# Second layer's straight path as one nest of arms with one packed control word; the gate of the token-order unit one unit earlier, its product by halves

## The chip, the core and the metric

The kernel runs on one core of one Trainium2 chip. The time is the device time in microseconds of one execution, as the median over runs; the trace is one profiled execution of the same program. The engines are named as in the trace: PE (TensorE matmuls), PEld (its weight loads), DVE (VectorE), ACT (ScalarE), POOL (GpSimd) and SP (SyncE, which issues DMAs). A "q" behind the name means the engine's sequencer, which runs ahead of the engine's array and carries out register loads, branches and semaphore waits.

## The reference

```
def reference(**kwargs):
    ...
    attn_out = _attn_ref(**attn_kwargs)              # 2 x 8 heads, 768 positions, width 64
    x = ... .reshape(B * S, H * D)                   # 1536 tokens x 512
    x = _moe_ref(x=x, **moe_kwargs)                  # max of three products, then w_out
    return _moe2_ref(x=x, **moe2_kwargs)

def _moe2_ref(x, w_skip, w_gate, w1, w2):
    do_compute = x @ w_skip > 0
    out = x.copy()
    xc = x[do_compute]
    logits = xc @ w_gate                             # 8 experts, one per token (argmax)
    ...
    for e in range(E):
        h = np.maximum(xc[mask] @ w1[e], 0.0)
        y[mask] = gate_w[mask, None] * (h @ w2[e])
    out[do_compute] = xc + y
    return out.astype(np.float32)
```

Attention with a window of 16 and pooled keys, a first layer ("max of three products"), and a second layer in which each token that is not skipped goes through one of eight experts. How many tokens an expert gets is known only when the chip has computed the logits.

## The kernel before

The first 293 us of the trace are attention and the first layer, in an order that a planner (`arrange`) worked out beforehand; the change leaves that order alone. What follows is the second layer. Routing (`route`, `route2`, `route3`) writes each token's number and gate into a table in HBM, sorted by expert; `counts` sums the experts' tokens on PE and leaves the sums in PSUM. From them `steps()` in `plan()` (lines 628 to 705, one-partition instructions on DVE, spread over the first unit) works out integers in the tile `ints`: how many units each expert has, where they begin, and two flags. `reg()` loads one integer from `ints` into a register, by default on all five engines.

Work is done in units. `pair(p, t)` takes 256 tokens through the expert whose weights lie in slot `p`: the first product `first(f)` (12 matmuls of 128x256 for each of 8 pieces), relu on ACT and its low part `htl` on DVE, and the second product `second(f)` (6 matmuls of 128x512). `begin` copies the token numbers and rows on POOL, `end` does the last sum on DVE and scatters rows with POOL's indirect DMA, `tail_x` and `tail` treat up to 32 tokens of a further expert beside a pair. `single(p, t)` takes 128 tokens: 24 matmuls of 128x512 into `ph[0]` and `ph[1]` (line 1187), four transposes for each half (`turn_h`, line 1193), 24 matmuls of 128x512 into `py[0]` (line 1221). With `dense` it is the token-order unit: the last 128 tokens in their own order (`turn_d`, `put_d` bring them in during the single before), with a gate per token that is zero for a token that other units have done. `begin_d` makes that gate: a DVE memset of `yq`, a PE matmul of `yq` with the bounds `lim` into `pq` (line 1155), five small DVE instructions. `end_d` multiplies by the gate and stores the result in two halves from SP.

The order is written out by hand (`manual_schedule`), and branches are taken by every engine on its own registers. After the first layer:

```
    with tc.If(EA > EARLY) as early2:      # two pairs of the largest expert, whose number is guessed
        with tc.manual_schedule():
            pair(0, 0, gen=steps())
            numbers()
            pair(0, 1)
    with early2.Else():
        ...                                # the same in two smaller forms
    ...
    with tc.manual_schedule():
        with tc.If(reg(ints[:, 6 * NE:6 * NE + 1], MAXT) > 0, preferred_fallthrough_block=False) as others:
            any_ranks()                    # general form, all eight experts
        with others.Else():
            most()                         # the straight path
```

The program joins behind `early2`, loads the flag for `others` and goes into one of two arms. In `most()` the two first expert counts are loaded into registers `VK[0]` and `VK[1]`; then come a pair, a second pair, a third if `VK[0] > 6` (within it a fourth if `VK[0] > 8`), a single if `VK[0]` is even, and, after a register load of the second flag, either a single followed by the token-order unit or a single alone. Each of these `If`s has its own join; the arm in which nothing is done there waits for its engine's earlier work and adds the skipped semaphore counts, since whoever waits later must find the same count on either way.

In the profiled execution the path is: `early2` true (pairs from 295 us and from 318.7), `most` (pairs from 342.2, 371.6 and 400.1; the condition `VK[0] > 6` holds, `VK[0] > 8` does not), no single in slot 0, then the single from 425.7 and the token-order unit from 440.9. By the source, a pair has 152 matmuls, a single 56 to 64, the token-order unit 56, and each has a weight load beside it.

Of the kernel before, what the change touches and what calls it, by code (L numbers as in the profile page):

```python
# [40 lines left out]
BIG = 1 << 20  # L41
NCH = 16
MAXT = NT
NRAW = 4
NCON = 293
NG9 = 10
# [99 lines left out]
def build(tc, a, out):  # L146
# [376 lines left out]
    def route2(u):  # L523
        acc = ACC[u]
        if u == NG - 1:
            ST["cnt"], ST["cntp"] = counts(ACC[NG], ST["part"])
        oh, ohb, do, w, tab = ST["rt", u]

        def be(z):
            return z.unsqueeze(1).broadcast_to([P, TPG, NE])  # L530
        pp = psM.tile([P, 512], F32, name="pm")
        for j in range(TPG):
            o = pp[:, j * NE:(j + 1) * NE]
            nc.tensor.matmul(o, tri, ohb[:, j, :], start=True, stop=False)
            for i in range(j):
                nc.tensor.matmul(o, ones, ohb[:, i, :], start=False, stop=False)
            nc.tensor.matmul(o, ones, acc, start=False, stop=True)
        ST["pp", u] = pp

    def route3(u):  # L540
        oh, ohb, do, w, tab = ST["rt", u]
        pp = ST["pp", u]

        def be(z):
            return z.unsqueeze(1).broadcast_to([P, TPG, NE])
        nc.vector.tensor_tensor(w, pp[:, :TPG * NE].rearrange("p (t e) -> p t e", e=NE), be(iocap), ALU.add)
        nc.vector.tensor_tensor(w, w, oh, ALU.mult)
        sl = tp.tile([P, TPG], F32, name="rsl")
        nc.vector.tensor_reduce(sl, w, AX.X, ALU.add)
        nc.vector.tensor_scalar(do, do, -float(BIG), float(BIG), ALU.mult, ALU.add)  # L550
        si = tp.tile([P, TPG], I32, name="rsi")
        nc.vector.tensor_tensor(si, sl, do, ALU.add)  # L552
        ST["si", u] = si

    def scatter(u, j):
        tab, si = ST["rt", u][4], ST["si", u]
# [3 lines left out]
    def counts(*accs):  # L560
        pc = psM.tile([P, 512], F32, name="pm")
        for i, acc in enumerate(accs):
            nc.tensor.matmul(pc[:1, i * NE:(i + 1) * NE], ones[:, :1], acc, start=True, stop=True)
        return [pc[:1, i * NE:(i + 1) * NE] for i in range(len(accs))]

    def count3():
        ST["c3"] = counts(ACC[NG - 1])[0]

    ONE = {}

# [30 lines left out]
    def plan():  # L601
# [5 lines left out]
        n, used, u1, rank, n0, nk, ek, bk, uk, pk, rb, xk, kc = T.values()  # L607
        dn, lim = pk, kc[:, :2]
        ci = mp.tile([1, NE], I32, name="p_ci")
        ints = mp.tile([1, 6 * NE + 2], I32, name="p_ints")  # L610
        ONE["lim"] = lim
        hq, hqt = M2["hq"]
        m, m2 = (z[:1, SEQ * NE:].rearrange("p (a b) -> p a b", b=NE) for z in (hq, hqt))
# [14 lines left out]
        def steps():  # L628
# [38 lines left out]
            V.tensor_copy(fs[:, 3:4], xk[:, 3:4])  # L667
            V.tensor_scalar(fs[:, 4:5], ONE["ge2"], -1.0, float(EARLY), ALU.mult, ALU.add)
            V.tensor_reduce(fr, fs, AX.X, ALU.max)
            V.tensor_copy(ints[:, 6 * NE:6 * NE + 1], fr)  # L670
            yield
            V.tensor_reduce(dn[:, 0:1], dn, AX.X, ALU.add)
            V.tensor_scalar(fr, fr, 0.0, None, ALU.is_equal)
            V.scalar_tensor_tensor(fr, nk[:, 1:2], 0.0, fr, ALU.is_gt, ALU.mult)
            V.tensor_tensor(fr, fr, dn[:, 0:1], ALU.mult)
            V.tensor_copy(ints[:, 6 * NE + 1:], fr)
            V.tensor_tensor(nk[:, 0:1], nk[:, 0:1], fr, ALU.subtract)
            V.tensor_tensor(dn[:, 1:2], nk[:, 0:1], ONE["ge2"], ALU.add)
            V.tensor_tensor(dn[:, 1:2], dn[:, 1:2], ONE["ge"], ALU.add)
            V.tensor_scalar(lim[:, 1:2], ek[:, 0:1], float(CAP), None, ALU.mult)  # L680
# [460 lines left out]
        end(2)  # L1141

    def turn_d():
        for c in range(KC1):
            o = slice(c * P, (c + 1) * P)
            nc.tensor.transpose(ptx[0][:, o], X2[NG - 1, TPG - 1][:, o], ident)  # L1146
# [3 lines left out]
        nc.scalar.copy(xth[:, :, :P], src)  # L1150
        nc.vector.tensor_tensor(xtl[:, :, :P], src, xth[:, :, :P].bitcast(F32), ALU.subtract)

    def begin_d():
        nc.vector.memset(yq[:1], 1.0)  # L1154
        nc.tensor.matmul(pq[:, :2], yq[:1], ONE["lim"], start=True, stop=True)  # L1155
        nc.vector.tensor_copy(gd[0], ST["si", NG - 1][:, TPG - 1:])  # L1156
        nc.vector.tensor_tensor(gd[1], gd[0], pq[:, 0:1], ALU.is_ge)
        nc.vector.tensor_tensor(gd[2], gd[0], pq[:, 1:2], ALU.is_lt)
        nc.vector.tensor_tensor(gd[1], gd[1], gd[2], ALU.mult)
        nc.vector.tensor_tensor(gd[1], gd[1], ST["rt", NG - 1][4][:, TPG - 1, 1:2].bitcast(F32), ALU.mult)  # L1160

    def end_d():
        rows = out[B * S - P:, :]
        nc.sync.dma_start(xr[1], rows)
        for z in (slice(0, DM // 2), slice(DM // 2, DM)):
            nc.vector.scalar_tensor_tensor(yo[0][:, z], py[0][:, z], gd[1], xr[1][:, z], ALU.mult, ALU.add)  # L1166
            nc.sync.dma_start(rows[:, z], yo[0][:, z])

    def single(p, t, spl=0, last=False, hr=HR, then=False, dense=False):
        if dense:  # L1170
            begin_d()
        else:
            begin(1)
        if spl:
            tail_x(spl)
        todo = list(range(NCH)) if spl else []
        pth = [ph[2], ph[0]]

        def splits(n):
            for _ in range(min(n, len(todo))):  # L1180
                split(todo.pop(0), 1 - p)

        def first(hf, ds):
            for d in ds:
                wh, wl = M2["w", p, 2 * d + hf]
                for n, (l, r) in enumerate(((xth, wh), (xth, wl), (xtl, wh))):
                    nc.tensor.matmul(ph[hf], l[:, d, :P], r, start=(d == 0 and n == 0), stop=(d == KC1 - 1 and n == 2))  # L1187
            if ds[-1] == KC1 - 1:
                nc.scalar.activation(hr[hf], ph[hf], AF.Relu)

        def turn_h(i):
            for c in range(4):
                nc.tensor.transpose(pth[i][:, c * P:(c + 1) * P], hr[i][:, c * P:(c + 1) * P], ident)  # L1193
            nc.scalar.copy(hth[i], pth[i])
            nc.vector.tensor_tensor(htl[i], pth[i], hth[i].bitcast(F32), ALU.subtract)

        first(0, [0, 1, 2, 3])
        splits(4)
        first(1, [0, 1])
        turn_h(0)  # L1200
        splits(2)
        first(1, [2, 3])
        splits(2)
        for f in range(8):
            wh, wl = M2["w", p, 8 + f]
            i, o = f // 4, f % 4 * P
            if f == 2:
                turn_h(1)
                if not last:
                    turn_x()  # L1210
                elif then:
                    turn_d()
                splits(4)
            if f == 3:
                if not last:
                    next_x(t + 2)
                elif then:
                    put_d()
                splits(4)
            for n, (l, r) in enumerate(((hth[i], wh), (hth[i], wl), (htl[i], wh))):  # L1220
                nc.tensor.matmul(py[0], l[:, o:o + P], r, start=(f == 0 and n == 0), stop=(f == 7 and n == 2))  # L1221
            if spl and f >= 4:
                tail(f - 4)
        if dense:
            end_d()
        else:
            end(1)

    def nothing(p, t, spl=0):
        if spl:  # L1230
# [7 lines left out]
        for c in range(NCH):  # L1238
            raw_load(c, reg(ints[:, NE + 1:NE + 2], NE - 1, **SP))

    take_x()
    with tc.If(EA > EARLY) as early2:
        with tc.manual_schedule():
            pair(0, 0, gen=steps())
            numbers()
            pair(0, 1)
    with early2.Else():
        ids("in2", reg(ONE["r0"], NROW - 2 * P, **SP))
        with tc.If(EA > 0) as early:
            with tc.manual_schedule():  # L1250
                pair(0, 0, gen=steps())
        with early.Else():
            for _ in steps():
                pass
            advance(row(1))
            turn_x()
            next_x(2)
        numbers()
    VK, EK, BK, LK, MR = {}, {}, {}, {}, {}

    def head(k, body, t):
# [14 lines left out]
    def run_rank(k):  # L1276
# [15 lines left out]
        if k + 1 < NE:  # L1292
            with tc.If(VK[k + 1] > 0):
                run_rank(k + 1)
    def most():

        for k in range(2):
            VK[k] = reg(ints[:, k:k + 1], MAXT + 1)
        b0, b1, l0 = (reg(ints[:, i * NE + k:i * NE + k + 1], 14, **SP) for i, k in ((2, 0), (2, 1), (3, 0)))
        MR[1], MR[2] = (reg(ints[:, 5 * NE + k:5 * NE + k + 1], NROW - P, **SP) for k in (1, 2))  # L1300
        e2 = reg(ints[:, NE + 2:NE + 3], NE - 1, **SP)
# [2 lines left out]
        for c in range(NCH):  # L1304
            raw_load(c, e2)
        pair(0, b0 + 2, FAST2)
        with tc.If(VK[0] > 6):
            pair(0, b0 + 3)
            with tc.If(VK[0] > 8):
                pair(0, b0 + 4)  # L1310
        with tc.If((VK[0] & 1) == 0):
            single(0, l0, hr=M2["raw"])
        with tc.If(reg(ints[:, 6 * NE + 1:], 1) > 0) as dense:
            single(1, b1 + 1, last=True, hr=M2["raw"], then=True)
            single(0, 0, last=True, hr=M2["raw"][2:], dense=True)
        with dense.Else():
            with tc.If(VK[1] > 1):
                single(1, b1 + 1, last=True, hr=M2["raw"])

    def any_ranks():  # L1320
        for k in range(NE):
# [2 lines left out]
                z[k] = reg(ints[:, i * NE + k:i * NE + k + 1], m, **SP)  # L1324
        run_rank(0)

    with tc.manual_schedule():
        with tc.If(reg(ints[:, 6 * NE:6 * NE + 1], MAXT) > 0, preferred_fallthrough_block=False) as others:
            any_ranks()
        with others.Else():  # L1330
            most()
    ctx.close()


# [61 lines left out]
```

## Time and profile before

| | us |
|---|---|
| median of 3 runs | 461.05 |
| lowest, highest | 458.27, 465.42 |
| the profiled execution | 461.48 |
| its span, first to last instruction | 459.6 |

The profiled execution's time is its span and 1.9 us around it. Of the span PE is busy 432.6 us (94%), DVE 245.7, ACT 197.2 and POOL 128.9. In rows of a timeline the columns are start, duration, engine, line, operation, output and inputs, and in brackets the idle time before and what ended it; starts are us from the span's beginning.

### The profile page before, as it was taken

What the parts mean: (1) busy time and instruction counts of PE and PEld (TensorE: products, weight loads), DVE (VectorE), ACT (ScalarE), POOL (GpSimd) and SP (SyncE); (2) the same over time, 40 slices, a digit from 0 to 9 for tenths busy, and PEclk for the clock granted to TensorE, in tenths of its full rate; (3) what the DMA queues carried; (4) which work ended last, traced back from release to release, by engine and by line L of the source; (5) the groups of instructions that cost most, each with busy time, mean ns of one, the idle gap of its engine ahead of it and who ended that gap; (6) DMA issues with size and microseconds to landing.
All of it is one profiled execution on the core that took longest, in us unless ns stands there. A gap on an engine that the chain in (4) does not pass through costs nothing. (4 is left out here: it accounts for less than half of the span.)

```text
span 459.6 us, 9467 instructions
## 1 busy us (share of the span) xinstructions
PE 432.6 (94%) x3426; PEld 387.2 (84%) x3426; DVE 245.7 (53%) x783; ACT 197.2 (43%) x522; POOL 128.9 (28%) x177
## 2 busy tenths in 40 slices
PE   7987799999999999999999999999998999998994
PEld 3556689899989899999999988998997889797773
DVE  4998999989963343445114174587136541313121
ACT  2799987756364472357221173211115511111210
POOL 2343453322121441423102511142224033232200
PEclk9999989999999999999999999999999999999899
DMA  8994625575525254220030290312941381010110
GB/s 245 269 271 167 239 103 183 181 244 202 178 85 193 100 189 118 49 82 22 3 134 5 61 348 7 137 11 79 345 121 51 117 297 49 25 50 2 48 49 30
DMA packets 28168, 58.46 MB, mean 127 GB/s; under 512 B 6163, under 2 KB 8723, under 8 KB 28104
## 3 DMA queue, kind: packets, MB, share of 16 engines
q1 hardware_dynamic: 25544, 51.71, 34.6%
q0 software_dynamic: 2560, 5.96, 4.1%
q8 instruction: 32, 0.52, 0.5%
q14 instruction: 32, 0.26, 0.2%
HBM read 48.16 MB, written 10.47 MB: 128 GB/s over the span
## 5 line engine op out<-in xcount | busy, mean ns | idle before, releaser
L367 PE MATMUL pm<-xh,wh 128*128 128x384 f32 x288 | 66.1, 349 | 3.2 <-DVE t L376 2.0
L367 PE MATMUL pm<-xh,wl 128*128 128x384 f32 x288 | 63.1, 339 | 0.0
L367 PE MATMUL pm<-xl,wh 128*128 128x384 f32 x288 | 63.1, 339 | 0.0
L367 PEld LDWEIGHTS pm<-xh,wh 128*128 128x128 f32 x288 | 49.4, 189 | 5.3 <-DVE t L376 2.5
L1106 ACT ACTIVATE hth<-ph 128x256 fp32r<-128x256 f32 x40 | 15.3, 384 | 89.5 <-PE ph L1103 72.2
L367 PEld LDWEIGHTS pm<-xh,wl 128*128 128x128 f32 x288 | 51.7, 190 | 0.5 <-DVE wl L360 0.5
L367 PEld LDWEIGHTS pm<-xl,wh 128*128 128x128 f32 x288 | 51.9, 190 | 0.0
L376 DVE TENSOR_TENSOR t<-pm,t 128x384 f32<-128x384 f32 x48 | 26.5, 553 | 37.8 <-PE pm L367 30.1
L1107 DVE SCALAR_TENSOR_TENSOR htl<-ph,hth 128x256 fp32r<-128x256 f32 x40 | 16.7, 422 | 55.5 <-ACT hth L1106 55.5
L287 POOL TENSOR_TENSOR pr<-pr,se 128x360 f32<-128x360 f32 x32 | 26.2, 823 | 68.9 <-DVE se L283 44.6
L394 PE MATMUL pm<-wh,h 128*128 128x262 f32 (+1 forms) x288 | 42.8, 288 | 1.3 <-ACT v L214 1.0
L277 ACT ACTIVATE pr<-pr,mx 128x120 f32<-128x120 f32 x96 | 36.6, 384 | 10.9 <-DVE mx L271 10.8
L384 POOL TENSOR_TENSOR h<-t,h 128x384 fp32r<-128x384 f32 x24 | 26.1, 1093 | 48.9 <-ACT h L381 47.4
L394 PEld LDWEIGHTS pm<-wh,h 128*128 128x128 f32 x288 | 37.9, 190 | 2.1 <-ACT v L214 1.3
L1115 PE MATMUL pm<-wh,htl 128*128 128x512 f32 x80 | 31.5, 394 | 1.3 <-DVE htl L1107 1.3
L1115 PE MATMUL pm<-wh,hth 128*128 128x512 f32 x80 | 31.8, 397 | 0.0
L1115 PE MATMUL pm<-wl,hth 128*128 128x512 f32 x80 | 31.4, 392 | 0.0
L557 POOL DMA_INDIRECT table<-rtab,rsi x12 | 11.9, 995 | 58.9 <-DVE rsi L552 38.9
L342 POOL TENSOR_SCALAR cx<-cx 128x512 f32<-128x512 f32 x24 | 18.3, 764 | 35.5 <-ACT cx L334 33.8
L736 POOL DMA_INDIRECT xn<-x2d,inx x14 | 14.9, 1063 | 46.0 <-DVE xm L1069 30.4
L381 ACT CAST h<-t 128x384 fp32r<-128x384 f32 x24 | 11.9, 513 | 35.2 <-DVE t L376 33.9
L1103 PE MATMUL ph<-xth,wh 128*128 128x256 f32 x160 | 26.4, 287 | 0.0
(338 smaller groups left out, 856.6 us busy)
## 6 DMA issues: line engine op xcount, KB each, us to landing
raw<-in_m SPq DMA_DIRECT2D x48, 256.0 KB
raw<-in_wx SPq DMA_DIRECT2D x22, 512.0 KB
kx<-in_kx SPq DMA_DIRECT2D x12, 360.0 KB
vx<-in_vx SPq DMA_DIRECT2D x14, 288.0 KB
qt<-in_qt SPq DMA_DIRECT2D x16, 192.0 KB
x2d<-raw SPq DMA_DIRECT2D x12, 256.0 KB
raw<-in_kt SPq DMA_DIRECT2D x7, 384.0 KB
raw<-in_vt SPq DMA_DIRECT2D x7, 384.0 KB
```

Source lines behind the costliest of these rows:

```text
L277: nc.scalar.activation(pr[:, t, :], pr[:, t, :], AF.Exp, bias=mx[:, t:t + 1], scale=-1.0, accum_out=se[:, t:t + 1])
L287: nc.gpsimd.tensor_tensor(pr, pr, se.unsqueeze(2).broadcast_to([P, TPG, KT]), ALU.mult)
L342: nc.gpsimd.tensor_scalar(x, x, HIGH, LOW, ALU.min, ALU.max)
L367: nc.tensor.matmul(ST["ch", u, f, j], l[j, f][:, c * P:(c + 1) * P], r[u][:, c, :], start=(cs[0] == 0 and n == 0), stop=(cs[-1] == KC1 - 1 ...
L376: nc.vector.tensor_tensor(ST["t1", u, f], ps, ST["t1", u, f], ALU.max)
L384: nc.gpsimd.tensor_tensor(HL[u, f], ST["t1", u, f], HH[u, f].bitcast(F32), ALU.subtract)
L394: nc.tensor.matmul(ps, l[u, f][:, t * P:(t + 1) * P], r[3, f][:, lo:hi], start=(part != 1 and n == 0), stop=(part != 0 and n == len(ops) - 1))
L736: nc.gpsimd.indirect_dma_start(out=xn[t], out_offset=None, in_=x2d, in_offset=bass.IndirectOffsetOnAxis(ap=inx[:, t, 0:1], axis=0), bounds ...
L1103: nc.tensor.matmul(ps, w[:, o:o + P], r[:, d, :], start=(n == 0), stop=(n == 3 * KC1 - 1))
L1106: nc.scalar.activation(hh, ps, AF.Relu)
L1107: nc.vector.scalar_tensor_tensor(hl, ps, 0.0, hh.bitcast(F32), ALU.max, ALU.subtract)
L1115: nc.tensor.matmul(py[i], l[:, o:o + P], r, start=(f == 0 and n == 0), stop=(f == 7 and n == 2))
```

## The change

`counts` returns one row of PSUM, and `route3` of the last group copies the sums into SBUF (one DVE copy). `steps()` no longer writes two flags but one word: the number of the largest expert's remaining units in the low five bits, 32 if the second expert has a full unit, 64 if the token-order unit is to run, 128 for the general form. The word is loaded once into all engines. The choice between `any_ranks` and `most` now stands inside the true arm of `early2`, without a join between; its Else part gets an `any_ranks` of its own. Inside `most` each `If` has its continuation within both arms, so the code of the later units is there several times: `last()` holds the single and the token-order unit (or the single alone), `odd()` a single and `last()`, or `last()` alone, and `odd()` stands behind the fourth pair, in the Else of the fourth, and in the Else of the third. The memset of `yq` moves into `turn_d`, the rest of `begin_d` becomes `gate_d` and is called behind `put_d` in the single before. The token-order unit's second product is done in two column halves of 256 (48 matmuls for 24): for f = 0 to 3 both halves by turns, then f = 4 to 7 of the first half, its sum and store, then the same for the second.

```diff
 ... (counts, count3: one row of PSUM is returned)
@@ route3
+        if u == NG - 1:
+            cs = w.rearrange("p t e -> p (t e)")[:1, :2 * NE]
+            nc.vector.tensor_copy(cs, ST["cnt"])
+            ST["cnt"], ST["cntp"] = cs[:, :NE], cs[:, NE:]
@@ steps
-            V.tensor_copy(ints[:, 6 * NE:6 * NE + 1], fr)
             yield
             V.tensor_reduce(dn[:, 0:1], dn, AX.X, ALU.add)
-            V.tensor_scalar(fr, fr, 0.0, None, ALU.is_equal)
-            V.scalar_tensor_tensor(fr, nk[:, 1:2], 0.0, fr, ALU.is_gt, ALU.mult)
-            V.tensor_tensor(fr, fr, dn[:, 0:1], ALU.mult)
-            V.tensor_copy(ints[:, 6 * NE + 1:], fr)
-            V.tensor_tensor(nk[:, 0:1], nk[:, 0:1], fr, ALU.subtract)
+            V.tensor_scalar(fs[:, 0:1], fr, 0.0, None, ALU.is_equal)
+            V.scalar_tensor_tensor(fs[:, 0:1], nk[:, 1:2], 0.0, fs[:, 0:1], ALU.is_gt, ALU.mult)
+            V.tensor_tensor(fs[:, 0:1], fs[:, 0:1], dn[:, 0:1], ALU.mult)
+            V.tensor_tensor(nk[:, 0:1], nk[:, 0:1], fs[:, 0:1], ALU.subtract)
+            V.tensor_scalar(fr, fr, 0.0, float(OTHER), ALU.is_gt, ALU.mult)
+            V.scalar_tensor_tensor(fr, fs[:, 0:1], float(DENSE), fr, ALU.mult, ALU.add)
+            V.tensor_scalar(fs[:, 1:2], nk[:, 1:2], 0.0, float(ONES), ALU.is_gt, ALU.mult)
+            V.tensor_tensor(fr, fr, fs[:, 1:2], ALU.add)
+            V.scalar_tensor_tensor(ints[:, 6 * NE:], nk[:, 0:1], 1.0, fr, ALU.mult, ALU.add)
@@ turn_d, begin_d, end_d
     def turn_d():
+        nc.vector.memset(yq[:1], 1.0)
         for c in range(KC1):
...
-    def begin_d():
-        nc.vector.memset(yq[:1], 1.0)
+    def gate_d():
         nc.tensor.matmul(pq[:, :2], yq[:1], ONE["lim"], start=True, stop=True)
...
+    halves = [slice(0, DM // 2), slice(DM // 2, DM)]
+
+    def second_d(z, f):
+        wh, wl = M2["w", 0, 8 + f]
+        h, o = f // 4, f % 4 * P
+        for n, (l, r) in enumerate(((hth[h], wh), (hth[h], wl), (htl[h], wh))):
+            nc.tensor.matmul(py[z][:, halves[z]], l[:, o:o + P], r[:, halves[z]],
+                             start=(f == 0 and n == 0), stop=(f == 7 and n == 2))
+
     def end_d():
         rows = out[B * S - P:, :]
         nc.sync.dma_start(xr[1], rows)
-        for z in (slice(0, DM // 2), slice(DM // 2, DM)):
-            nc.vector.scalar_tensor_tensor(yo[0][:, z], py[0][:, z], gd[1], xr[1][:, z], ALU.mult, ALU.add)
-            nc.sync.dma_start(rows[:, z], yo[0][:, z])
+        for z, cs in enumerate(halves):
+            for f in range(4, 8):
+                second_d(z, f)
+            nc.vector.scalar_tensor_tensor(yo[0][:, cs], py[z][:, cs], gd[1], xr[1][:, cs], ALU.mult, ALU.add)
+            nc.sync.dma_start(rows[:, cs], yo[0][:, cs])
@@ single
-        if dense:
-            begin_d()
-        else:
+        if not dense:
             begin(1)
...
+            if dense and f == 4:
+                end_d()
+                return
             if f == 3:
                 if not last:
                     next_x(t + 2)
                 elif then:
                     put_d()
+                    gate_d()
                 splits(4)
+            if dense:
+                for z in range(2):
+                    second_d(z, f)
+                continue
@@ most
-    def most():
-        for k in range(2):
-            VK[k] = reg(ints[:, k:k + 1], MAXT + 1)
+    def most(w):
...
-        with tc.If(VK[0] > 6):
+        def last():
+            with tc.If((w & DENSE) > 0, preferred_fallthrough_block=True) as dense:
+                single(1, b1 + 1, last=True, hr=M2["raw"], then=True)
+                single(0, 0, last=True, hr=M2["raw"][2:], dense=True)
+            with dense.Else():
+                with tc.If((w & ONES) > 0):
+                    single(1, b1 + 1, last=True, hr=M2["raw"])
+
+        def odd():
+            with tc.If((w & 1) > 0) as one:
+                single(0, l0, hr=M2["raw"])
+                last()
+            with one.Else():
+                last()
+
+        with tc.If((w & (ONES - 1)) > 5, preferred_fallthrough_block=True) as four:
             pair(0, b0 + 3)
-            with tc.If(VK[0] > 8):
+            with tc.If((w & (ONES - 1)) > 7, preferred_fallthrough_block=True) as five:
                 pair(0, b0 + 4)
-        with tc.If((VK[0] & 1) == 0):
-            single(0, l0, hr=M2["raw"])
-        with tc.If(reg(ints[:, 6 * NE + 1:], 1) > 0) as dense:
-            single(1, b1 + 1, last=True, hr=M2["raw"], then=True)
-            single(0, 0, last=True, hr=M2["raw"][2:], dense=True)
-        with dense.Else():
-            with tc.If(VK[1] > 1):
-                single(1, b1 + 1, last=True, hr=M2["raw"])
+                odd()
+            with five.Else():
+                odd()
+        with four.Else():
+            odd()
@@ the end of build
+    with tc.If(EA > EARLY, preferred_fallthrough_block=True) as early2:
+        with tc.manual_schedule():
+            pair(0, 0, gen=steps())
+            numbers()
+            pair(0, 1)
+            word = reg(ints[:, 6 * NE:], 2 * OTHER - 1)
+            with tc.If(word >= OTHER, preferred_fallthrough_block=False) as others:
+                any_ranks()
+            with others.Else():
+                most(word)
+    with early2.Else():
...
+        numbers()
         with tc.manual_schedule():
             any_ranks()
```

## Rows read from the trace of the kernel before

**Rows 1.** The page: engines' busy time, and one of its two instruction queues

```profile
PE 432.6 (94%) x3426; PEld 387.2 (84%) x3426; DVE 245.7 (53%) x783; ACT 197.2 (43%) x522; POOL 128.9 (28%) x177
...
q8 instruction: 32, 0.52, 0.5%
```

**Rows 2.** Timeline, DVE at the end of the first pair

```profile
318.25 1.43 DVE L1078 SCALAR_TENSOR_TENSOR yo<-pm,ic,xr 128x512 f32<-128x512 f32 x2 [0.71 <-PE pm L1115]
```

**Rows 3.** Timeline, SP, DVE and PE around the entry into `most`

```profile
341.07 0.75 SPq L1015 DMA_DIRECT2D mi<-table  x1
...
341.68 1.43 DVE L1078 SCALAR_TENSOR_TENSOR yo<-pm,ic,xr 128x512 f32<-128x512 f32 x2 [0.71 <-PE pm L1115]
...
347.75 0.21 DVE L1021 TENSOR_SCALAR mo<-mi,con 128x1 int32<-128x1 int32 x1 [4.64 <-PE pm L1115]
...
347.94 1.08 DVE L1107 SCALAR_TENSOR_TENSOR htl<-ph,hth 128x256 fp32r<-128x256 f32 x3
...
348.41 0.50 PE L1115 MATMUL pm<-wh,htl 128*128 128x512 f32 x1 [1.30 <-DVE htl L1107]
```

**Rows 4.** By line (count, duration min/median/max in ns, first and last start): early2's branches, loads

```profile
L1242 DVEq COMPARE_BRANCH  x2: 55/56/57, 296.0 to 342.4; - x2
...
L712 DVEq EVENT_SEMAPHORE  x5: 21/50/50, 346.0 to 346.9; - x5
...
L1242 PEldq COMPARE_BRANCH  x2: 92/198/304, 293.4 to 339.2; - x2
```

**Rows 5.** By line, PE's sequencer: the branches behind the last pair and the last

```profile
L1309 PEldq COMPARE_BRANCH  x2: 190/262/333, 420.7 to 424.0; - x2
...
L1311 PEldq COMPARE_BRANCH  x1: 438/438/438, 424.4 to 424.4; - x1
...
L1313 PEldq COMPARE_BRANCH  x2: 77/1736/3394, 425.4 to 450.7; - x2
```

**Rows 6.** Timeline, PE from the last pair to the first single

```profile
423.42 0.39 PE L1115 MATMUL pm<-wh,htl 128*128 128x512 f32 x1
425.65 0.47 PE L1187 MATMUL ph<-wh,xth 128*128 128x512 f32 x1 [1.84 <-DVEq L1311]
```

**Rows 7.** A stretch: us, PE busy (instructions), granted clock, DMA share, GB/s

```profile
426.80:430.10 3.30, 3.30 (x10) 0.50 0.06 25
```

**Rows 8.** The chain that ended last: start, us, what

```profile
425.65 5.97 PE ph L1187 x18
...
441.23 4.42 PE ph L1187 x18
...
449.30 4.19 PE pm L1221 x18
```

**Rows 9.** Timeline, DVE and PE around the gate

```profile
435.98 0.69 DVE L1195 TENSOR_TENSOR htl<-ph,hth 128x512 fp32r<-128x512 f32 x1 [2.53 <-ACT hth L1194]
...
436.24 0.40 PE L1221 MATMUL pm<-mw_11h,hth 128*128 128x512 f32 x1
...
439.44 0.39 PE L1221 MATMUL pm<-mw_15h,htl 128*128 128x512 f32 x1
...
440.63 0.17 DVE L1154 MEMSET yq<- 1x128 f32 x1
...
440.85 0.38 PE L1155 MATMUL pm<-p_kc,yq 1*128 1x2 f32 x2 [1.03 <-DVE mo L1156]
441.16 0.51 PE L1187 MATMUL ph<-wh,xth 128*128 128x512 f32 x1
```

**Rows 10.** Stretch, matmuls of line 1103 alone: us, PE busy (instructions), clock, DMA

```profile
318.75:323.02 4.27, 4.27 (x36) 1.00 0.72 204
```

**Rows 11.** Timeline, the end: PE, DVE, SP

```profile
453.08 0.40 PE L1221 MATMUL pm<-wh,htl 128*128 128x512 f32 x1
...
453.51 0.87 DVE L1166 SCALAR_TENSOR_TENSOR yo<-pm,mo,xr 128x256 f32<-128x256 f32 x2 [2.87 <-PE pm L1221]
454.02 1.27 SPq L1167 DMA_DIRECT2D out<-yo  x2
```

More of the change, by code (lines that the diff above doesn't have):

```diff
@@ L43 @@
 MAXT = NT
+ONES, DENSE, OTHER = 32, 64, 128
 NRAW = 4
@@ L525, in route2 @@
         if u == NG - 1:
-            ST["cnt"], ST["cntp"] = counts(ACC[NG], ST["part"])
+            ST["cnt"] = counts(ACC[NG], ST["part"])
         oh, ohb, do, w, tab = ST["rt", u]
@@ L563, in counts @@
             nc.tensor.matmul(pc[:1, i * NE:(i + 1) * NE], ones[:, :1], acc, start=True, stop=True)
-        return [pc[:1, i * NE:(i + 1) * NE] for i in range(len(accs))]
+        return pc[:1, :NE * len(accs)]
     def count3():
-        ST["c3"] = counts(ACC[NG - 1])[0]
+        ST["c3"] = counts(ACC[NG - 1])
     ONE = {}
@@ L609, in plan @@
         ci = mp.tile([1, NE], I32, name="p_ci")
-        ints = mp.tile([1, 6 * NE + 2], I32, name="p_ints")
+        ints = mp.tile([1, 6 * NE + 1], I32, name="p_ints")
         ONE["lim"] = lim
@@ L1223, in single @@
                 tail(f - 4)
[L1224 to L1227, printed above, removed]
+        end(1)
     def nothing(p, t, spl=0):
@@ L1239, in numbers @@
             raw_load(c, reg(ints[:, NE + 1:NE + 2], NE - 1, **SP))
[L1241 to L1258, printed above, removed]
     VK, EK, BK, LK, MR = {}, {}, {}, {}, {}
@@ L1325, in any_ranks @@
         run_rank(0)
-    with tc.manual_schedule():
-        with tc.If(reg(ints[:, 6 * NE:6 * NE + 1], MAXT) > 0, preferred_fallthrough_block=False) as others:
+    take_x()
+    with tc.If(EA > EARLY, preferred_fallthrough_block=True) as early2:
[9 more added lines that the diff above has]
+    with early2.Else():
+        ids("in2", reg(ONE["r0"], NROW - 2 * P, **SP))
+        with tc.If(EA > 0) as early:
+            with tc.manual_schedule():
+                pair(0, 0, gen=steps())
+        with early.Else():
+            for _ in steps():
+                pass
+            advance(row(1))
+            turn_x()
+            next_x(2)
+        numbers()
+        with tc.manual_schedule():
             any_ranks()
-        with others.Else():
-            most()
     ctx.close()
```

## The prediction

> **What bounds the kernel now.** I read the page first: PE is busy for 432.6 of the span's 459.6 us [rows 1], so only what leaves PE standing, or makes it slower, can be won. Next I read the waits of PE and followed each one behind 293 us, where the change begins, in the timeline. There are three places that the change touches.
>
> The first is the entry into `most`. PE stands 1.30 us for the low part `htl` of the first piece; DVE makes it only at 347.94, behind `tail_x` at 347.75 [rows 3]. DVE had ended its last work before that at 341.68 + 1.43 = 343.11. The load of `mi` that `tail_x` reads was issued at 341.07 and its issue took 0.75 us [rows 3], so a transfer is not what DVE lacked for all of 4.64 us. The rows by line show what it did: its branch of line 1242, from the end of early2's true arm over the Else part, starts at 342.4, and its next instruction (a semaphore check of line 712) not before 346.0 [rows 4]: 3.6 us for one jump. Then come the waits of the join, the flag and `VK`.
>
> The second is the end of the last pair. The next matmul could follow 423.42 after 0.23 us (18 matmuls of 128x512 take 4.19 us [rows 8], 0.233 each), at 423.65; it starts at 425.65 [rows 6]. That is 2.00 us, spent in joins (PE has to drain before it may add skipped counts), branches and a flag's load. [...]
>
> The third is the gate. From 439.44 + 0.23 = 439.67 to 441.16 PE does nothing but the tiny matmul of line 1155, which waits for DVE's memset, which stands behind the single's last sum [rows 9]: 1.49 us.
>
> **The entry.** The jump over the Else part, the join's waits and the loads of `VK` go; one word is loaded and the branch to `others` falls through to `most`. DVE then comes from 343.11 to `tail_x` in about 0.6 us (nearest rows: a branch of 0.06 and the rest of 346.0 to 347.75 halved, [rows 3, 4]). SP's load for `mi` also comes earlier, since SP no longer loads `VK` before it. Piece 0 of `htl` is wanted after the second matmul of line 1115, at 347.1 (348.41 - 1.30), so more than 2 us remain. I take the whole stall: -1.30. Bounds: 0 and -1.30.
>
> **The planner.** One DVE copy is added in `route3` and three one-partition instructions net in `steps`, at 0.17 us each (nearest row: the one-partition memset [rows 9]), 0.5 us within the first pair. DVE's idle 0.71 us ahead of its sum at 318.25 [rows 2] covers it. Without that cover it would be +0.5. I take 0.
>
> **The end of the last pair.** This decides. No join and no load is left between pair and single, so PE's sequencer need not drain. But `VK[0]` is 7 here (its conditions > 6 true, > 8 false, even false), so the word's low bits are 6, and the path goes through the Else of `five` and the Else of `one`: two taken jumps, over code that the change has made longer. By the source the jump of `five` passes one pair (152 matmuls), one single (64) and twice `last()` (62 + 80 + 56 = 198): 612 matmuls and as many weight loads, 1,224 instructions. The jump of `one` passes 64 + 198 = 262 matmuls, 524 instructions.
>
> What does such a jump cost on PE? Three taken jumps are short: over early2's Else (about 330 instructions) 0.304 us [rows 4], over a pair (304 instructions) 0.333, over a single (some 130) 0.438; the far one at the end, over the general form, 3.394 [rows 5]. On DVE the jump over the Else part, some 165 instructions by the source, already cost 3.6 us. The new jumps lie between the short ones and the far one. As an estimate, 6,852 matmuls and loads in 32 instruction packets [rows 1], if that queue is PE's, make 214 in a packet: the short jumps reach 1.5 packets ahead, the new ones 5.7 and 2.4. A price that steps from 0.4 to 3.4 rather than growing with distance fits code that is there or has to be fetched. I take 3.39 for both, keep 0.33 to 0.44 as the other bound, and allow that only one is far.
>
> The sequencer reaches the condition of `five` where it now reaches that of line 1309, at 420.7 [rows 5], 2.95 us ahead of the array. With two far jumps: 420.7 + 3.39, 0.25 for the next condition (now 425.4 to 425.65 from the last condition to the matmul, [rows 5, 6]), 3.39 again, 0.25: the single starts at 428.0. PE stands 428.0 - 423.65 = 4.35 us where it stood 2.00: +2.35. With both short the sequencer is through at about 422.0, before the array is free: -2.00. With one far, at 425.0: -0.65.
>
> The clock: it fell behind an idle of 1.84 us [rows 6], not behind 1.30 and 1.03 [rows 3, 9]. [...]
>
> **The gate, one unit earlier.** It takes the 1.49 us away. In the single before, the memset now stands on DVE behind `htl` of the second half, 435.98 + 0.69 [rows 9]; it starts at about 436.6, and the matmul of line 1155 follows a memset's start by 0.22 us (440.63 to 440.85): 436.8. PE would have gone on with f = 3 at 436.24, so it stands 0.57 us there, and the gate's matmul itself takes 0.31 (440.85 to 441.16). Sum: 0.57 + 0.31 - 1.49 = -0.61. Queued behind PE's wait are the matmuls of f = 3, whose inputs are there; behind DVE's memset `xtl`, wanted 4 us later. The first matmul of the token-order unit needs neither `ic` nor the scatter behind `end`. Bounds: -1.18 (no wait) to 0.
>
> **Halves.** 36 matmuls of 128x256 took 4.27 us [rows 10], 0.119 each: 48 take 5.69, where 24 of 0.233 took 5.59: +0.10. At the end DVE began 0.43 us after the last matmul's start and worked 0.87 us on two halves [rows 11]. Only one half, 0.44, is left there, and the last matmul has half the columns (0.12 less): -0.55. Together -0.45. The first store lies earlier by twelve matmuls; the second one's issue, landing and the end remain. Bounds: -0.8 (the issue of one store, of 1.27 us for two, shorter too) to +0.1.
>
> **Sum.** -1.30 + 0 + 2.35 + 0 - 0.61 - 0.45 = -0.01 against the profiled 461.48: 461.5. That run lies 0.43 above the median of 461.05, so on the scale of medians 461.0; because the clock's bound on the long side is open while the idle is long, I lean up a little: **461.3 us**.
>
> **Rivals.** *Both jumps short.* Then -1.30 - 2.00 - 1.55 - 0.61 - 0.45 = -5.91: 455.1. For it: three PE jumps were short. Against: none was longer than 330 instructions, and DVE's of 165 was far.
>
> [...]
>
> *One jump far.* -1.30 - 0.65 - 0.61 - 0.45 = -3.01, and with an idle of 1.35 us the clock may hold (-1.55): 456.5 to 458, say 457.2. For it: the jump of `one` is the shorter, 2.4 packets by the estimate. Against: it comes 0.25 us behind a fetch, when nothing further can be there yet.
>
> *Slower: each level of the nest ends with a jump of its own.* All engines have to get from inside `dense`, `one`, `five`, `four`, `others` and `early2` to the end. If levels are left one by one, each far jump costs 3.39 us [rows 5] in the chain behind the last store, and one extra decides: 464.7, three extra 471.5. Against: now `dense` stands within `others`, and PE has one jump there, at 450.7 [rows 5].
>
> *The change does nothing*, because the straight path isn't taken, can't be: the same inputs go through `most`.
>
> **How the numbers follow.** Two far jumps 0.68, one far 0.14, both short 0.12, end jumps 0.06. The likeliest one's own range is 459 to 464.5 (clock +1.55, gate 0, and that medians of three runs here differ by a microsecond or two, runs from 458.27 to 465.42). With the one-jump case the range is **456.0 to 464.5**; what is left out is 0.12 + 0.06. Two per cent, about what a measurement of this kernel tells from no change, is 9.2 us, below 451.8 or above 470.3: only several end jumps get there. Faster 0.02, same 0.95, slower 0.03.
>
> **What would show it.** Right: PE's branches at `five` and `one` near 3.4 us each, 4 us or more of idle ahead of the first matmul of the single, clock 0.50 behind it; no stall of PE at line 1115 behind 342 us; a wait of about 0.6 us at the gate's matmul and none between the two last units; one DVE piece of 0.44 us behind the last matmul. Wrong: branches of 0.4 us and single matmuls that follow the pair at once (then 455), DVE still late at the entry (+1.30), or more than one branch of some 3 us on SP behind the last store.

## The result, and the profile after

The changed kernel takes 463.09 us (median of 22 runs, 460.83 to 466.69), the kernel before beside it 460.79 us (22 runs; one of them took 2354 us, which moves a median by next to nothing). The ratio is 1.0063 with a 95% interval of 1.0039 to 1.0086: some 2 to 4 us slower, and within 2%. The forecast was 461.3 us, 456.0 to 464.5.

The profiled execution took 464.36 us, with a span of 462.6. From the first matmul of the first pair of the second layer to the last matmul it needs 1.8 us more than before (160.25 us for 158.45), and behind the last matmul 0.7 less (5.37 for 6.10). The other 1.9 of the 3.0 us by which the span is longer lie ahead of the first pair, which starts at 296.92 instead of 295.03. That start lies between 292.35 and 298.00 in the other profiles below, with the same first layer, so I don't ascribe it to the change. By stages, from the starts of PE's matmuls in both timelines:

| stage | before, us | after, us | difference |
|---|---|---|---|
| two pairs of early2 | 47.13 | 47.24 | +0.11 |
| first pair of `most` | 29.41 | 27.85 | -1.56 |
| second pair | 28.57 | 27.96 | -0.61 |
| third pair, to its last matmul's start | 23.28 | 23.29 | +0.01 |
| from there to the single's first matmul | 2.23 | 5.97 | +3.74 |
| single, to the token-order unit's first matmul | 15.51 | 15.52 | +0.01 |
| token-order unit, to the end of the span | 18.43 | 17.81 | -0.62 |

What PE waits for from 290 us on (waits view of the kernel after: who waited for whom, us in total, times, longest) is now two things. The entry's 1.3 us for `htl` is gone, as is a wait of 0.4 in the second pair's tail, and one wait is new:

```profile
PE ph L1204 <- issue: 5.6, 1, 5.6
PE pm L1163 <- DVE yq L1152: 0.4, 1, 0.4
```

"issue" is time in which the array waits for nothing that the profile shows. So the next view is the sequencer's branches, by line (kernel after; count, duration min/median/max in ns, first and last start). `five` is line 1327, `one` 1319, `dense` 1311:

```profile
L1327 PEldq COMPARE_BRANCH  x1: 3446/3446/3446, 420.6 to 420.6; - x1
...
L1319 PEldq COMPARE_BRANCH  x1: 4632/4632/4632, 424.2 to 424.2; - x1
...
L1311 PEldq COMPARE_BRANCH  x2: 77/1994/3910, 429.0 to 455.1; - x2
```

Two jumps, 3.45 and 4.63 us, one right behind the other, against 0.33 and 0.44 in [rows 5]. The array has its last matmul at 423.26 and its next at 429.23, where it was 423.42 and 425.65 in [rows 6] (timeline, PE):

```profile
423.26 0.39 PE L1123 MATMUL pm<-wh,htl 128*128 128x512 f32 x1
429.23 0.76 PE L1204 MATMUL ph<-wh,xth 128*128 128x512 f32 x1 [5.58 <-issue]
```

The low clock of [rows 7] is there again and lasts longer. These stretches of the kernel after show us, PE busy (instructions), the loads and the other engines, then the granted clock, DMA share and GB/s:

```profile
423.70:429.20 5.50, 0.00 (x0) 0.00 (x0) 0.74 (x2) 0.00 (x0) 1.52 (x3) 0.77 0.20 57
429.30:433.50 4.20, 4.20 (x10) 3.33 (x11) 0.00 (x0) 0.00 (x0) 1.00 (x1) 0.50 0.19 70
433.60:444.90 11.30, 10.85 (x54) 8.72 (x53) 2.65 (x9) 2.86 (x5) 0.87 (x3) 1.00 0.01 3
```

The clock is at 0.50 for the ten first matmuls behind the idle. In the chain of work that ended last (start, us, what), the first 18 matmuls of the single take 6.39 us for 5.97 in [rows 8]. Those of the token-order unit have 4.21 for 4.42, but a piece of the chain starts with its first matmul only where PE stood idle before it, and otherwise up to 0.17 us later, where the piece before it ends. From the first matmul's start to that of the transposes behind the 18, the single's take 6.23 us for 5.81 and the token-order unit's 4.22 for 4.32; below I compare by these.

```profile
423.65 5.58 issue
429.23 6.39 PE ph L1204 x18
...
444.92 4.21 PE ph L1204 x18
...
452.87 4.32 PE pm L1176 x36
```

At the entry (timeline, DVE), the first instruction of `tail_x` (line 1029) follows the pair's last sum after 0.22 us, where it was 4.64 in [rows 3]:

```profile
343.68 1.43 DVE L1086 SCALAR_TENSOR_TENSOR yo<-pm,ic,xr 128x512 f32<-128x512 f32 x2 [0.70 <-PE pm L1123]
...
345.33 0.21 DVE L1029 TENSOR_SCALAR mo<-mi,con 128x1 int32<-128x1 int32 x1 [0.22 <-DVE yo L1086]
```

### The profile page after: what moved, and what is told of

It is laid out like the page before. It is cut to its first block, busy times and chain, and to the rows that moved or that the text cites. A ratio compares the mean times of both kernels' runs of the same rounds, so it can differ in the third digit from the quotient of the medians.

```text
span 462.6 us, 9488 instructions
## 1 busy us (share of the span) xinstructions
PE 434.4 (94%) x3446; PEld 390.4 (84%) x3450; DVE 248.8 (54%) x787; ACT 197.6 (43%) x522; POOL 127.9 (28%) x177
## 4 chain that ended last, share of the span: by engine, by line
PE 70%; DVE 9%; DMA 6%; issue 5%; ACT 5%; POOL 2%; SPq 1%; POOLq 0%; ACTq 0%
PE pm L368 19%; PE ph L1111 13%; PE pm L1123 12%; PE pm L395 11%; PE ph L1204 3%; ACT pr L278 3%; DMA raw<-in_m 3%; DMA raw<-in_kt 2%; PE pt L293 2%; PE po L306 2%; PE sc L259 2%; DVE cx L349 1%; PE pm L1176 1%; PE ptx L731 1%; DVE cx L353 1%
```

## The experiments

All times are given as ratios to the kernel before, which ran on the same chip beside them (its medians were 460.12 us in the first four, 460.70 in the others), with 95% intervals. The single's idle and the 18 matmuls behind it, from the first one's start to that of the transposes, are read from each kernel's timeline. Every kernel is traced once.

| kernel | median, us | ratio (interval) | branch at `five`, `one` on PE, us | idle ahead of the single, us | next 18 matmuls, us |
|---|---|---|---|---|---|
| before | 460.79 | 1 | 0.33, 0.44 | 1.84 | 5.81 |
| changed | 463.09 | 1.0063 (1.0039 to 1.0086) | 3.45, 4.63 | 5.58 | 6.23 |
| e1, both fall through | 453.75 | 0.9869 (0.9826 to 0.9912) | 0.07, 0.07 | 0 | 4.20 |
| e2, `five` far | 455.82 | 0.9918 (0.9883 to 0.9953) | 3.68, 0.08 | 1.26 | 4.28 |
| e3, `one` far | 455.52 | 0.9912 (0.9881 to 0.9943) | 0.07, 3.75 | 1.32 | 4.28 |

### Both arms laid out for falling through (e1)

```diff
-            with tc.If((w & 1) > 0) as one:
+            with tc.If((w & 1) > 0, preferred_fallthrough_block=False) as one:
...
-            with tc.If((w & (ONES - 1)) > 7, preferred_fallthrough_block=True) as five:
+            with tc.If((w & (ONES - 1)) > 7, preferred_fallthrough_block=False) as five:
```

> The changed kernel with the arms of `five` and `one` laid out so that the path taken here falls through; the same instructions run. Theory (two far jumps of PE's sequencer, 3.45 and 4.63 us, leave PE idle and the idle costs clock behind it): the first matmul of the single follows the pair at once (idle 5.58 us to about 0), no branch over 0.5 us on PE before the end, granted clock 1.0 behind it, so the 18 first matmuls take 4.2 us for 6.39; 463.1 - 5.5 - 2.2 = about 455.4, 0.988 of the kernel before. Rival A (the idle belongs to the nest itself, its longer code or its semaphores): idle stays above 3 us, 461 to 463. Rival B (the clock falls at this place whatever the idle): idle gone, but 18 matmuls still near 6 us, about 457.4.

Measured: 453.75 us, 0.9869. The branches are at 0.07 us (by line, PE's sequencer), the single's first matmul follows the pair's last after 0.23 us (timeline), and the clock stays at 1.00 (stretch, columns as above):

```profile
L1327 PEldq COMPARE_BRANCH  x1: 71/71/71, 418.3 to 418.3; - x1
...
L1319 PEldq COMPARE_BRANCH  x1: 67/67/67, 418.5 to 418.5; - x1
```

```profile
420.93 0.39 PE L1123 MATMUL pm<-wh,htl 128*128 128x512 f32 x1
421.16 0.39 PE L1204 MATMUL ph<-wh,xth 128*128 128x512 f32 x1
```

```profile
421.20:425.50 4.30, 4.30 (x21) 3.44 (x20) 0.91 (x2) 0.60 (x1) 1.68 (x3) 1.00 0.17 61
```

The same instructions in another layout: so the idle belongs to the jumps, not to the nest's code or its semaphores (rival A), and the clock falls because of the idle (rival B falls). Idle 5.97 - 0.23 = 5.74 and clock 6.23 - 4.20 = 2.03 make 7.8 us of the 8.2 by which the stretch from first pair to last matmul is shorter (160.25 to 152.03); the other 0.4 lie in the two pairs of early2 (47.24 to 46.84).

### One far jump at a time (e2, e3)

e2 is e1's second edit undone, e3 its first undone.

> The changed kernel with only the arms of `one` laid out for falling through; the jump at `five` stays far (26,059 instructions on PE). Theory: the jump starts at 420.6 and takes 3.45 us, two conditions follow, the single's first matmul at about 424.6: idle 1.0 us instead of 5.6; if the clock holds after such a short idle 463.1 - 4.5 - 2.2 = 456.4, if it falls 458.5. Rival A (idle belongs to the nest): 461 to 463. A rival on the price of a second jump (4.63 because it comes right behind the first one's fetch): here the single jump takes 3.4.

> The changed kernel with only the arms of `five` laid out for falling through; the jump at `one` stays, and now it alone is far (26,605 instructions on PE, as its Else part lies behind the general form). Theory: it starts at about 420.9 and takes 3.4 us, not the 4.63 of the changed kernel, if 4.63 was the price of coming right behind another fetch; first matmul at about 424.7, idle 1.1 to 1.3; 456.4 with the clock held, 458.5 without. If 4.63 belongs to this jump whatever precedes it: idle 2.4, about 458 to 460. Rival A: 461 to 463.

Measured: 455.82 and 455.52 us, 0.9918 and 0.9912, so rival A (461 us or more) falls in both. Branches by line, first e2's, then e3's:

```profile
L1327 PEldq COMPARE_BRANCH  x1: 3681/3681/3681, 418.4 to 418.4; - x1
...
L1319 PEldq COMPARE_BRANCH  x1: 83/83/83, 422.2 to 422.2; - x1
```

```profile
L1319 PEldq COMPARE_BRANCH  x1: 3750/3750/3750, 419.1 to 419.1; - x1
```

Alone, the jump of `one` costs 3.75 us; 0.15 us behind that of `five` it costs 4.63. Nine other far jumps of PE, in the kernels before and after, e1, e2, e3 and e8, among them the last one of each of the first five, took 3.39 to 3.92 us, so 4.63 stands apart by 0.7 us or more. Coming right behind another far jump is the likely reason, but not shown outright, as it is not the same jump: in the changed kernel it passes some 540 instructions (counted in the compiled program), in e3 26,605, and no run holds its place fixed. And one far jump costs the array only 1.3 us, since the sequencer starts it 2.4 to 2.7 us ahead of the array's last matmul; the second one has no such lead and stands in the open in full. In both kernels the clock held behind the 1.3 us (granted clock 1.00, 18 matmuls in 4.28).

### A longer arm that is never run, in the kernel before (e8)

```diff
             with tc.If(VK[0] > 8):
                 pair(0, b0 + 4)
+                single(0, l0, hr=M2["raw"])
```

> The kernel before with a single added behind the fourth pair, in the arm that is never run here: PE's taken jump at that If goes over 437 instructions instead of 308, and nothing else that runs changes. [...]

The time put on record for it is 464 to 465.5 us, 1.007 to 1.010, with the lengthened jump at the 3.4 us of the far one in [rows 5]. Measured: 464.35 us, 1.0079 (1.0048 to 1.0110). Branches by line of that kernel (1309 is the lengthened `If`: its jump, 3.75 us, and the short one out of its empty arm; 1312 is the `If` of the single behind it):

```profile
L1309 PEldq COMPARE_BRANCH  x2: 190/1970/3750, 421.3 to 425.2; - x2
...
L1312 PEldq COMPARE_BRANCH  x1: 2704/2704/2704, 425.6 to 425.6; - x1
```

From 308 to 437 instructions passed, the price goes from 0.33 to 3.75 us: a step. The jump behind it, over some 135 instructions as before, goes from 0.44 to 2.70: I had not expected that. It starts at 425.6, some 0.5 us behind the end of the far one (421.3 + 3.75); why it took longer there this run doesn't show. Idle 4.72 us, 18 matmuls 6.29 us. A price that grows with the distance from 0.33 us would have left the time at 1.000, and falls.

So 437 instructions were too far here, and 308 were not. Whether distance alone decides, or also where the branch and its target lie in the code, no run here shows.

### The gate and the halves without the nest (e4)

The kernel before, with `turn_d`, `gate_d`, `second_d`, `end_d` and the lines of `single` from the changed one.

> The kernel before with the gate one unit earlier and the product by halves, its branches left as they were. Theory (these two parts are worth what the sum says and don't hang on the nest): gap between single and token-order unit gone (1.49 us), a wait of 0.45 to 0.6 and the gate's own 0.3 inside the single: -0.6; end of the last matmul to the end of the last sum shorter by a half of 0.43 us: -0.45. Together -1.05, 0.9977 of the kernel before; the idle before the single stays 2.0 to 2.2 us. Rival (the gap comes back elsewhere, as a wait for the gate's values or for the transposed rows): no difference, or the gap stands at another place.

Measured: 458.25 us, 0.9979 (0.9949 to 1.0010), by itself not told from 1. In its timeline the gap between the units is gone, and PE waits inside the single:

```profile
434.74 0.17 DVE L1144 MEMSET yq<- 1x128 f32 x1
...
434.96 0.38 PE L1155 MATMUL pm<-p_kc,yq 1*128 1x2 f32 x2 [0.45 <-DVE yq L1144]
```

From the transposes behind the single's first 18 matmuls to the token-order unit it takes 9.23 us for 9.70, and from the transposes behind that unit's first 18 matmuls to the end 13.37 for 14.11.

It also showed something that I did not look for: its idle ahead of the single is that of the kernel before (2.23 us from matmul to matmul in both), but the 18 matmuls behind it took 4.29 us at clock 1.00, where the kernel before has 5.81. So the same idle cost clock in one execution and not in another. The ten runs of this one kernel split the same way: seven take 458.1 to 458.7 us at a granted clock of 0.991 to 0.998 over the whole run, three 461.4 to 462.6 at 0.987 or 0.988.

### The join put back behind the first branch (e6)

```diff
-    with tc.If(EA > EARLY, preferred_fallthrough_block=True) as early2:
+    with tc.If(EA > EARLY) as early2:
...
             pair(0, 1)
-            word = reg(ints[:, 6 * NE:], 2 * OTHER - 1)
-            with tc.If(word >= OTHER, preferred_fallthrough_block=False) as others:
-                any_ranks()
-            with others.Else():
-                most(word)
     with early2.Else():
...
         numbers()
-        with tc.manual_schedule():
-            any_ranks()
+    with tc.manual_schedule():
+        word = reg(ints[:, 6 * NE:], 2 * OTHER - 1)
+        with tc.If(word >= OTHER, preferred_fallthrough_block=False) as others:
+            any_ranks()
+        with others.Else():
+            most(word)
```

(on e1)

> The changed kernel with both arms falling through, and the choice of the general form put back behind a join of the first branch, as in the kernel before (VectorE again jumps over the Else part, some 176 instructions). Theory (VectorE's jump of 3.6 us makes it late with the low part): PE stands 1.3 us at the product of the first piece, and the wait of 0.4 in the tail's matmuls comes back if it hangs on it: +1.3 to +1.7 over the version without the join, 455.0 to 455.5. Rival (the flags' loads, not the join's jump, made VectorE late; one word for three values then already helps): +0.3 or less, 454.0.

Measured: 457.18 us, 0.9926 (0.9897 to 0.9955). VectorE jumps at 343.0 and its next semaphore check (line 720) starts at 347.1, some 4.1 us. The checks there take 0.02 to 0.05 us each, where one of SP's on that line, which waits, takes 17.02, so it is the jump that takes the time (by line, then timeline):

```profile
L1343 DVEq COMPARE_BRANCH  x2: 55/56/57, 297.2 to 343.0; - x2
...
L720 DVEq EVENT_SEMAPHORE  x4: 21/50/50, 347.1 to 347.4; - x4
```

```profile
348.05 0.21 DVE L1029 TENSOR_SCALAR mo<-mi,con 128x1 int32<-128x1 int32 x1 [4.31 <-PE ph L1111]
...
348.71 0.50 PE L1123 MATMUL pm<-wh,htl 128*128 128x512 f32 x1 [0.97 <-DVE htl L1115]
```

The first pair of `most` takes 29.09 us, for 27.84 in e1: +1.25. One word instead of several loads, with the jump left, keeps most of the stall: 0.97 us of the 1.30, and the pair is 0.3 us shorter than the 29.41 of the kernel before. The other part of the expectation fell: the wait of 0.4 us in the second pair's tail (line 1049) is there in this kernel, but also in the next two without the join, and not in e8, which has it. It goes with the chip: e1, e2, e3 and e8 ran on one and have none of it, e4 and e6, e7 and e9 ran on another and all have it. Why is open; the -0.61 of the second pair in the table is it, and no gain of the change. From first pair to last matmul e6 takes 1.87 us more than e1 by the trace, 1.25 here and the rest in that wait; the ratios differ by more (0.0057, 2.6 us), with intervals that overlap and from two chips.

### The memset earlier (e7)

```diff
     def turn_d():
-        nc.vector.memset(yq[:1], 1.0)
...
     def single(...):
...
+        if then:
+            nc.vector.memset(yq[:1], 1.0)
```

(on e1)

> The changed kernel with both arms falling through, and the memset for the gate at the start of the single instead of behind the second half's low part. Theory (the gate's matmul waits for nothing else than that memset): PE's stall of 0.45 to 0.5 us at line 1163 goes, about 0.3 of its own stays; 453.3, 0.986 of the kernel before. Rival (the matmul then waits for the rows' transposes or for the bounds): stall stays 0.3 or more, 453.7.

Measured: 453.98 us, 0.9852 (0.9824 to 0.9880). No wait at the gate's matmul (here line 1162) is left; the single takes 12.93 us for e1's 13.45, so 0.52 us. In the time this is not told from e1. It and e1 have the lowest ratios, 1.3 and 1.5% below the kernel before; of the others, all but e8 and e4 are below it too, none by 2%.

### The second product undivided (e9)

On e1, with `end_d` behind all 24 matmuls of 512 columns into `py[0]`, as in the kernel before.

> The changed kernel with both arms falling through, and the token-order unit's second product undivided as in the kernel before (24 matmuls of 512 columns, both sums behind the last). Theory: PE ends 0.1 us earlier, and VectorE works 0.87 us behind the last matmul instead of 0.48; the span from the second half's transposes to the end is 0.4 to 0.5 us longer; 454.2. Rival (the store's issue or landing sets the end, so that the earlier first store gains more, or the split gains nothing): 0 or over 0.8 us.

Measured: 454.61 us, 0.9899 (0.9854 to 0.9943), not told from e1 by the time. From the token-order unit's first matmul to the end: 18.15 us, for 17.88 in e1. The chain of e9, then that of e1:

```profile
440.97 4.19 PE pm L1237 x18
...
445.58 0.47 DVE yo L1183
```

```profile
440.82 1.46 PE pm L1176 x12
...
442.71 4.30 PE pm L1176 x36
...
447.04 0.48 DVE yo L1185
```

So against e1 the halves are worth 0.27 us: 445.16 to the span's end at 451.10 is 5.94 us behind the last matmul, 447.01 to 452.49 is 5.48, hence -0.46; the narrower matmuls cost 0.11 behind the last transposes and some 0.08 ahead of them.

## Why the prediction was right, and where it was not

**What bounds it, and which case.** Right. The case forecast as likeliest, two far jumps at `five` and `one`, is what the branches of the kernel after show. The time came out 1.8 us above the 461.3 and inside the range, with some luck: the range was left open upwards for the clock and the gate, and what used it up was the price of the second jump, which had no bound on that side. The rivals' own times held where an experiment made them real: "both short" was put at 455.1, and e1's ratio gives 0.9869 x 460.79 = 454.8; "one far" at 457.2, and e2 and e3 give 457.0 and 456.7. Extra end jumps did not come: PE has one at 455.1, and SP's last branch of line 1311 took 0.04 us. What SP has there and I had not is three semaphore instructions of line 1319 ahead of that branch, 0.23 us, which neither the kernel before nor e4 has.

**The entry, -1.30.** Right in cause and a little small: the pair is 1.56 us shorter. e6 puts 1.25 of it down to the join and its jump, and e6 has the other 0.3 already, with one load for several.

**The planner, 0.** Right: the two pairs of early2 take 47.24 us for 47.13, and 46.84 or 46.85 both in e4 and e8, which have the old planner, and in e1, e2 and e3, which have the new one.

**The jumps, +2.35.** Two far jumps was right, and this term was mis-sized: the idle grew by 3.74. I priced both jumps by the one row of 3.39 us [rows 5]. `five` cost 3.45, `one` 4.63, most likely as it follows another far jump at once (alone, in e3, 3.75): 1.24 of the missing 1.39. I had written a reason down ("when nothing further can be there yet") as an argument against one rival, and not priced it; that code has to be fetched at a far jump is an inference of mine from the prices, which no run shows. One distance was wrong too: counted by the source I had `five` pass 1,224 instructions (and `one` 524, which is near), but the compiled program lays its Else part behind the whole general form, 26,059 instructions away (counted in the compiled program). It made no difference: 437 instructions in e8 cost 3.75 us.

**The clock, 0, with a bound of +1.55.** Inside the bound: the sum has 0, as if the low stretch stayed as it was, and the longer idle made the 18 matmuls 0.42 us slower than before (6.23 for 5.81). But the base was softer than I took it. I read "1.84 us of idle brings the fall, 1.30 doesn't" from one execution; e4 shows the same 1.84 without the fall. The kernel before is no firmer: over the 42 of its runs beside the experiments the granted clock is 0.979 to 0.998, while no run of the changed kernel is above 0.990. Over many runs the longer idle may so cost more clock than this pair of profiles shows. The 1.55 itself is what the single's first 18 matmuls take above those of the token-order unit by the chain (5.97 and 4.42 in [rows 8]); from start to start it is 1.49 (5.81 for 4.32). No run shows a second such stretch: the longest idle, 5.58 us, has 6.23 behind it, and the 4.72 of e8 6.29; without an idle, in e1, they take 4.20, which is 1.61 less.

**The gate, -0.61.** Right in place and cause, and near in size: PE stands 0.92 us from 440.26 (last matmul 440.03 + 0.23) to 441.18, for 1.49, that is -0.57, and the memset behind `htl` is what it waits for:

```profile
440.00 0.69 DVE L1212 TENSOR_TENSOR htl<-ph,hth 128x512 fp32r<-128x512 f32 x1 [2.48 <-ACT hth L1211]
...
440.65 0.17 DVE L1152 MEMSET yq<- 1x128 f32 x1
...
440.87 0.38 PE L1163 MATMUL pm<-p_kc,yq 1*128 1x2 f32 x2 [0.45 <-DVE yq L1152]
441.18 0.50 PE L1246 MATMUL pm<-mw_11h,hth 128*128 128x512 f32 x1
```

The matmuls of the second product around this wait take 0.15 us more than without one, so that from their first start to the token-order unit it is 5.27 us for 5.69, -0.42. I left out that the unit behind it, no longer started after an idle, does its 18 matmuls in 4.22 us for 4.32: 0.10 more. Together -0.52.

**Halves, -0.45.** Right in direction; the size depends on what they are held against. Between e9 and e1 it is -0.27: the end gains 0.46 where I had 0.55, and the matmuls cost 0.19 where I had 0.10. Between the kernel before and e4 it is -0.74, and most of the difference lies in the second store's issue, which at the end of the kernel before took 0.81 us. At the end of the kernel after, one sum of 0.48 us stands behind the last matmul, where [rows 11] had 0.87, and the stores' issues take 0.37 and 0.34 us (timeline, DVE; then by line, SP, the kernel after and the kernel before):

```profile
457.21 0.48 DVE L1185 SCALAR_TENSOR_TENSOR yo<-pm,mo,xr 128x256 f32<-128x256 f32 x1 [0.94 <-PE pm L1176]
```

```profile
L1186 SPq DMA_DIRECT2D out<-yo x2: 338/352/366, 456.3 to 457.7; - x2
```

```profile
L1167 SPq DMA_DIRECT2D out<-yo x2: 366/590/813, 454.0 to 454.5; - x2
```

Undivided, the issues are not constant: from the first one's start to the second one's end they took 1.27 us in the kernel before and 0.84 in e9. My bound of -0.8 for the case of a shorter issue held. In the changed kernel -0.52 is left (13.59 us for 14.11), as the three semaphore instructions stand in the same end.

**The sum.** With the measured terms: +0.11 (planner) - 1.56 (entry) + 3.74 (idle) + 0.42 (clock) - 0.52 (gate) - 0.52 (halves and end) = +1.67, where I had -0.01. The two profiles differ by 1.08 from the first pair on, because the second pair's wait of 0.61 is in one of them alone; the medians differ by 2.30 (1.8 to 4.0 by the interval). The change takes away 2.6 us at three places and puts 4.2 us of jumps and clock in one.

## What to carry to other kernels

When a branch is moved or its arms grow, ask for each engine which arm is laid out next to it: the arm that is run should fall through, and a taken jump over 437 matmuls and loads or more must be priced at the 3.4 to 3.9 us it took on PE here, not at the 0.33 of one over 308. Most of one such jump is hidden if the sequencer is ahead of the array (1.3 us of 3.7 showed); a second one right behind it was not, and took more (4.63 us, where it took 3.75 alone). Duplicating the continuation into both arms removes the joins, but it also moves the arms apart, so set the fall-through side at every level of the nest, not at the outer ones alone; which side is right depends on the data, and e1 is tuned for the path of this input.

## What the runs showed of the hardware that was not expected

- A taken jump on PE is 0.33 us over 308 instructions and 3.75 us over 437; at 26,000 it is 3.45 to 3.75: beyond the step the price doesn't grow with the distance.
- A jump right behind a far one took more: 4.63 us instead of 3.75 for a far one, 2.70 instead of 0.44 for a short one.
- The other engines pay at `five` too, each 2.4 to 3.7 us (ACT 419.7 to 422.1, DVE 423.8 to 427.5, POOL 429.4 to 432.1 between this branch and the next condition, each 0.1 us in e1), without PE waiting for them here.
- The clock fell behind an idle of 1.84 us in one execution and not in another; it fell behind 4.7 and 5.6 us and held behind 1.3. At a granted clock of 1.00 an idle still costs a little: in the kernel before the second matmul behind 1.30 us of it (348.41) starts 0.34 us after the first and behind 1.84 us (425.65) 0.32, where 0.23 is usual, and 18 matmuls take 4.28 us in e2 and e3 for 4.20 in e1.
- SP's issues of the two last stores, one right behind the other, took 1.27 us from start to end in the kernel before (0.37 and 0.81 us for the two) and 0.84 in e9.
